# Packed attention and a gated convolution on one core: batch 0's first layer in two halves, its convolution off TensorE, more steps on GpSimd, other fillers, another order

## The chip, the cores and the metric

The kernel runs on one core of a Trainium2 chip, as one program in one launch. The metric is device time in microseconds, from the first instruction to the last. The kernel before takes 399.19 us (median of 3 runs, 398.37 to 400.52).

## The reference

Eight batches; attention has 8 heads of 576 positions and 64 channels, and 32 packed queries per head. What is computed, cut to what matters:

```python
p_packed = softmax(p @ k.T / 8) @ v          # 32 packed rows per head
x = softmax(q @ p_packed.T / 8) @ p_packed   # 576 rows per head, joined to 576 x 512 per batch
h = relu(x @ w_in)                           # 512 -> 1024
c = conv_w[0] * h[s-1] + conv_w[1] * h[s] + conv_w[2] * h[s+1]
out = (h * sigmoid(c)) @ w_out               # 1024 -> 512
```

q, k, v and p are float32; w_in, conv_w and w_out reach the kernel as 64-bit floats, which it rounds itself.

## The kernel before, in words

**Tiling.** The work is cut into 16 groups `g` of 4 heads (two per batch). For a group, `attention(g)` scores the packed queries against the keys, takes a softmax (`a1`), multiplies by `v`, turns the result (`ppT`), scores it against the queries and takes a second softmax in the tile `s2` (the profile writes `s`): VectorE turns it out of PSUM, takes maxima, subtracts them, ScalarE takes the exponential, VectorE sums, divides (a multiplication by the reciprocal) and turns it again. `packed_weight(b, hf)` multiplies the packed rows by `w_in`, so that the second attention product and the first layer become one product. `ffn1(b, j)` is that product for batch `b` and one of 8 blocks `j` of 128 channels. Then come a ReLU into a buffer `hbuf` (three of them), the three taps of the convolution, a tanh and a product into `hgt`. `ffn2(m)` multiplies 128 rows (36 tiles `m`, 4.5 per batch) by `w_out`; it first splits `hgt` into `xhi` and `xlo`.

**Two ways to multiply.** A float32 product on TensorE takes four passes over its columns, which the profile records as two matmuls. A split product writes each factor as a high and a low part in the one-pass format fp32r and adds three products (hi·hi, lo·hi, hi·lo). Before the change batch 0's first layer is float32 (tiles `a2f` and `gwf`, 4 instructions of 288 columns per `j`), and the other batches are split (`a2hi`, `a2lo`, `ghi`, `glo`, 12 instructions of 288 columns). In batch 0 the convolution of `j` = 0 is done by TensorE against three diagonal matrices (L903; GpSimd builds these, L497); all others are a tap on ScalarE (L927, one on VectorE, L923), two on VectorE (L929, L933), the tanh on ScalarE (L937) and the product on VectorE (L939). For the first two batches `glo` comes from TensorE: it adds minus the high part to the PSUM tile (L843).

**Who does what.** Names in the set `ON_DVE` put a step on VectorE where the function `either` would put it on ScalarE. Of the additions that round the weights, those not named there are done by GpSimd (L412, 512 columns each), each held by a dependency until the vector instruction before it in the program has ended.

**Order.** The string `ORDER` holds two characters per step: which stream's next step is issued. A planner made it beforehand from durations written into each `Step`. All engines work through their own queues in that order. `Flow` replays the plan while the program is built, and where it foresees that TensorE would wait, before the first tiles of the second layer, it puts in fillers (`warm(n)`, tile `idle`): matmuls whose result nobody reads. Loads are issued by SP, those of the first keys by ScalarE.

## Time and profile before

| | |
|---|---|
| median of 3 runs | 399.19 us |
| the profiled execution | 400.12 us; its span in the profile 398.3 us |
| TensorE (PE) busy | 390.3 us, 98% |
| VectorE (DVE) busy | 339.1 us, 85% |
| ScalarE (ACT) busy | 268.1 us, 67% |
| GpSimd (POOL) busy | 13.6 us, 3% |
| mean granted TensorE clock | 0.994 of full speed |

The 1.8 us between the span and the execution's time lie outside the recorded instructions. PE counts as busy from the start of a matmul to its modelled end, and matmuls overlap in the pipeline, so two further readings are needed: how long a run of matmuls lasts in the chain of work that ended last, and how busy the other engines are in the same stretch. A line such as L1058 is a line of the kernel before.

### The profile page before, as it was taken

The numbers are of one execution on the slowest core, as the hardware profiler recorded it, in microseconds if no ns is written. First come the engines' busy times: TensorE is split into PE (matmuls) and PEld (weight loads), VectorE is DVE, ScalarE is ACT, GpSimd is POOL, SyncE is SP. The second block draws the span as 40 slices with busy tenths as digits, with TensorE's granted clock in tenths as the row PEclk, the third lists the DMA queues.
The fourth block names the chain that finished last, engine by engine and source line by source line (L and its number), as shares of the span: only waits on it lengthen the run. The fifth ranks groups of instructions, "written<-read, shape, count | busy, mean of one in ns | idle before, by whom it ended". The sixth has DMA issues, their size and how long they took to land.

```text
span 398.3 us, 8049 instructions
## 1 busy us (share of the span) xinstructions
PE 390.3 (98%) x3281; PEld 310.6 (78%) x3281; DVE 339.1 (85%) x494; ACT 268.1 (67%) x430; POOL 13.6 (3%) x23
## 2 busy tenths in 40 slices
PE   6999999999999999999999999999999999999996
PEld 6767666678679789787788887989688878998885
DVE  3799999999999999999999899989976995887120
ACT  2599999887757577676846866757756667666221
POOL 1013112100000000000000000000000000000000
PEclk8999999999999999999999999999999999999999
DMA  8998899976989562976679626160000101001111
GB/s 274 358 371 256 199 309 149 185 105 106 168 153 152 107 96 54 143 140 94 156 108 157 162 28 156 19 114 26 28 26 28 53 2 53 28 0 54 53 53 54
DMA packets 157540, 47.60 MB, mean 120 GB/s; under 512 B 145460, under 2 KB 148788, under 8 KB 157504
## 3 DMA queue, kind: packets, MB, share of 16 engines
q1 hardware_dynamic: 157104, 46.41, 55.7%
q10 hardware_dynamic: 368, 0.66, 0.6%
q8 instruction: 26, 0.43, 0.5%
q14 instruction: 10, 0.08, 0.1%
q0 software_dynamic: 32, 0.02, 0.0%
HBM read 37.64 MB, written 9.44 MB: 118 GB/s over the span
## 4 chain that ended last, share of the span: by engine, by line
PE 88%; DMA 4%; DVE 3%; ACT 2%; SPq 1%; issue 1%; ACTq 0%; DVEq 0%
PE fo L1058 40%; PE big L880 23%; PE big L626 4%; PE sm L1058 4%; PE big L1008 4%; PE big L815 3%; PE sm L719 2%; PE big L710 2%; DMA hgt<-in_k_dram 2%; DMA p<-in_p_dram 1%; PE big L606 1%; SPq L676 1%; DMA out_dram<-o 1%; DVE hgt L929 1%; PE big L903 1%
## 5 line engine op out<-in xcount | busy, mean ns | idle before, releaser
L1058 PE MATMUL fo<-wo_hi,xhi 128*128 128x512 f32 x240 | 96.4, 402 | 0.4 <-ACT o L1073 0.4
L1058 PE MATMUL fo<-wo_lo,xhi 128*128 128x512 f32 x240 | 93.9, 391 | 0.0
L1058 PE MATMUL fo<-wo_hi,xlo 128*128 128x512 f32 x240 | 93.7, 390 | 0.0
L897 ACT ACTIVATE hbuf<-big 128x576 f32<-128x576 f32 x64 | 41.7, 653 | 40.5 <-PE big L880 40.3
L929 DVE SCALAR_TENSOR_TENSOR hgt<-hbuf,cw,hgt 128x576 f32<-128x576 f32 x63 | 50.5, 808 | 13.0 <-ACT hgt L927 12.2
L1031 DVE TENSOR_TENSOR xlo<-hgt,xhi 128x1024 fp32r<-128x1024 f32 (+1 forms) x38 | 41.6, 1102 | 18.3 <-ACT xhi L297 18.1
L1058 PEld LDWEIGHTS fo<-wo_hi,xhi 128*128 128x128 f32 x240 | 45.0, 188 | 14.4 <-issue 3.9
L937 ACT ACTIVATE hgt<-hgt 128x576 f32<-128x576 f32 x63 | 42.7, 683 | 18.4 <-DVE hgt L933 18.3
L1058 PEld LDWEIGHTS fo<-wo_hi,xlo 128*128 128x128 f32 x240 | 45.1, 188 | 10.1
L1058 PEld LDWEIGHTS fo<-wo_lo,xhi 128*128 128x128 f32 x240 | 45.1, 188 | 7.3
L933 DVE SCALAR_TENSOR_TENSOR hgt<-hbuf,cw,hgt 128x576 f32<-128x576 f32 x63 | 50.3, 805 | 0.6
L880 PE MATMUL big<-a2hi,ghi 128*128 128x288 f32 x224 | 49.7, 303 | 0.0
L927 ACT ACTIVATE hgt<-hbuf,cw 128x576 f32<-128x576 f32 x62 | 47.9, 777 | 1.0
L939 DVE SCALAR_TENSOR_TENSOR hgt<-hgt,hbuf 128x576 f32<-128x576 f32 x63 | 46.6, 750 | 2.0 <-ACT hgt L937 1.7
L880 PE MATMUL big<-a2lo,ghi 128*128 128x288 f32 x224 | 47.7, 294 | 0.0
L880 PE MATMUL big<-a2hi,glo 128*128 128x288 f32 x224 | 47.5, 293 | 0.0
L297 ACT CAST xhi<-hgt 128x1024 fp32r<-128x1024 f32 (+1 forms) x38 | 36.1, 954 | 10.9 <-PE fo L1058 4.9
L880 PEld LDWEIGHTS big<-a2hi,ghi 128*128 128x128 f32 x224 | 37.8, 188 | 6.0 <-ACT glo L297 0.5
L880 PEld LDWEIGHTS big<-a2hi,glo 128*128 128x128 f32 x224 | 35.8, 188 | 0.0
L880 PEld LDWEIGHTS big<-a2lo,ghi 128*128 128x128 f32 x224 | 35.8, 188 | 0.0
L1073 ACT COPY o<-fo 128x512 f32<-128x512 f32 x30 | 17.5, 584 | 22.2 <-PE fo L1058 18.4
L815 PE MATMUL big<-w_in_sb,ppT 64*32 64x512 f32 (+1 forms) x288 | 17.4, 547 | 0.5 <-ACT qT L297 0.5
(128 smaller groups left out, 551.8 us busy)
## 6 DMA issues: line engine op xcount, KB each, us to landing
out_dram<-o SPq DMA_DIRECT2D x35, 256.0 KB, 2.3
k<-in_k_dram SPq DMA_DIRECT2D x48, 144.0 KB, 4.1
q<-in_q_dram SPq DMA_DIRECT2D x48, 144.0 KB, 4.0
v<-in_v_dram SPq DMA_DIRECT2D x40, 128.0 KB, 3.1
hgt<-in_moe_w_in_dram SPq DMA_DIRECT2D x3, 1024.0 KB, 12.4
v<-in_v_dram SPq DMA_DIRECT2D x6, 512.0 KB, 9.4
hgt<-in_moe_w_out_dram SPq DMA_DIRECT2D x3, 1024.0 KB, 5.5
hgt<-in_q_dram SPq DMA_DIRECT2D x2, 576.0 KB, 6.8
```

Of the source, the lines that this page charges most:

```text
L297: nc.scalar.copy(out=out, in_=in_)
L815: nc.tensor.matmul(out=t[32 * c : 32 * c + 32, gg, :].rearrange("c (a f) -> c a f", f=DFF // 4), lhsT=grp[NG * b + gg]["ppT"][r, 32 * c : ...
L880: nc.tensor.matmul(out=t[:, hf, :SH], lhsT=w[:, gg, js], rhs=x[:, hf * SH : (hf + 1) * SH], start=n == 0, stop=n == (1 if b in F1F else 3) ...
L897: nc.scalar.activation(out=inner, in_=t[:, :, :SH], func=AF.Relu, scale=0.5)
L927: nc.scalar.activation(out=d, in_=h[:, 1 : S + 1], func=AF.Copy, scale=cw[:, NJ + j : NJ + j + 1])
L929: nc.vector.scalar_tensor_tensor(out=d, in0=h[:, 0:S], scalar=cw[:, j : j + 1], in1=d, op0=ALU.mult, op1=ALU.add)
L933: nc.vector.scalar_tensor_tensor(out=d, in0=h[:, 2 : S + 2], scalar=cw[:, 2 * NJ + j : 2 * NJ + j + 1], in1=d, op0=ALU.mult, op1=ALU.add)
L937: nc.scalar.activation(out=d, in_=d, func=AF.Tanh)
L939: nc.vector.scalar_tensor_tensor(out=d, in0=d, scalar=1.0, in1=h[:, 1 : S + 1], op0=ALU.add, op1=ALU.mult)
L1031: nc.vector.tensor_tensor(out=lo[:, js, o], in0=src[:, js], in1=hi[:, js, o].bitcast(F32), op=ALU.subtract)
L1058: nc.tensor.matmul(out=t, lhsT=x[:, c, :], rhs=w[:, c % 2, :], start=c + i == 0, stop=c == NJ - 1 and i == 2)
L1073: nc.scalar.copy(out=o, in_=t)
```

## The change

It does six things:

1. `F1F` becomes empty: batch 0's first layer is split as in the other batches. Each `j` has 12 one-pass instructions in place of 4 four-pass ones; `ghi` and `glo` are also made for batch 0 (8 more one-pass matmuls of 256 columns against `minus`, 4 more copies to `glo`), and so are `a2hi` and `a2lo` of its two groups.
2. `CONV_PE` becomes empty: the convolution of batch 0's `j` = 0 goes the way of all others; the 6 float32 matmuls and GpSimd's diagonal matrices are gone.
3. A set `ON_POOL` names the steps that GpSimd does: 8 additions of weights, 9 of the 16 subtractions and 13 of the 16 products in the second softmax, and 9 of the `xlo` subtractions of 1024 columns.
4. `ON_DVE` is another set: 8 ReLUs, 12 taps (before: one), `xhi` casts of 7 whole and 4 half tiles and 4 casts to `a2hi` are among what VectorE takes from ScalarE.
5. A filler is one single-pass matmul of 512 columns on zeros, in place of a float32 one of 128 columns on the identity. There are 29 of them; before there were 17.
6. `ORDER` is new, from a planner with other load times (three for the loads of weights, others for `v`) and a rule for turns between GpSimd and VectorE.

The new functions for quarter tiles (`quad_...`, `packed_again`) are not called, since `QUAD_K` and `QUAD_Q` are empty. Cut to its core, the diff is:

```diff
-    "3636363636000302360003356z073a0e046z05040a0534717101050a050c050c3b06340h3473093b050c0634700h053470050c0508347305"
+    "36350002003603013636036y346y3604076z366z0534040a0505700a3470340606050c053a3b0e09050h0c05340576720c05083b720d0h34"
...
-    FILL_NS, FILL_COLS, MARGIN = 216, 512, 100
+    FILL_NS, FILL_COLS, MARGIN = 226, 512, 100
...
-    ON_DVE = {"a1T0", "add20", "add21", "add30", "add40", "add50", "add51", "add70", "kT10", "kT15", "kT20", "qT00", "r0", "tap01"}
+    ON_DVE = {"gh000", "hi1", "hi10", "hi15", "hi5", "kT15", "qT05", "qT10", "r0", "relu45", "relu54", "relu64", "relu66", "relu67", "relu70", "relu73", "relu77", "tap02", "tap03", "tap31", "tap36", "tap40", "tap46", "tap56", "tap60", "tap64", "tap67", "tap70", "tap77", "x190", "x210", "x220", "x240", "x250", "x270", "x310", "x320", "x340"}
+    ON_POOL = {"add00", "add01", "add10", "add11", "add21", "add41", "add60", "add61", "mul0", "mul10", "mul11", "mul13", "mul14", "mul2", "mul3", "mul4", "mul5", "mul6", "mul7", "mul8", "mul9", "sub10", "sub13", "sub14", "sub3", "sub4", "sub5", "sub7", "sub8", "sub9", "xl20", "xl240", "xl260", "xl30", "xl330", "xl50", "xl60", "xl70", "xl80"}
-    F1F = (0,)
+    F1F = ()
-    CONV_PE = (0,)
+    CONV_PE = ()
...
+    nc.vector.tensor_copy(out=zeros, in_=stage[:, :128])
...
-            nc.tensor.matmul(out=t[:, :128], lhsT=ident, rhs=ident, start=True, stop=True)
+            nc.tensor.matmul(
+                out=t,
+                lhsT=zeros,
+                rhs=zeros.unsqueeze(1).broadcast_to([128, 4, 128]),
+                start=True,
+                stop=True,
+            )
...
+    def early_turn(key):
+        n = int("".join(c for c in key if c.isdigit()))
+        return n >= (40 if key[:3] == "add" else 4) or key[:2] == "xl"
...
+    def tensor_tensor(key, **kw):
+        if key not in ON_POOL:
+            nc.vector.tensor_tensor(**kw)
+            return
+        old = [i for i in nc.cur_bb.bb.instructions if i.engine == mybir.EngineType.DVE][-2 if early_turn(key) else -1]
+        added = nc.gpsimd.tensor_tensor(**kw)
+        tc.add_manual_dep(
+            added.ins,
+            old.name,
...
-        yield Step("SP", 2650 if i < 3 else 3500, after=after, sets=[("wd", i)])
+        yield Step("SP", (2650, 2650, 2650, 3200, 3200, 3600, 3600, 3600)[i], after=after, sets=[("wd", i)])
...
-        yield Step("DVE", 669)
-        nc.vector.tensor_tensor(
-            out=s3, in0=s3, in1=sm.unsqueeze(2).broadcast_to([128, SB, NP]), op=ALU.mult
+        yield either_pool(f"mul{g}", 1161, 669)
+        tensor_tensor(
+            f"mul{g}", out=s3, in0=s3, in1=sm.unsqueeze(2).broadcast_to([128, SB, NP]), op=ALU.mult
         )
```

**TensorE at the start.** These are its first instructions before: the seven early ones on `stage`, fillers, the turning of the first keys and queries, the first score (`kT,pT`) and the turning of the first softmax (`a_...`).

```order
L267 MATMUL idle<-stage 128x128 x7
L262 MATMUL idle<-ident 128x128
L606 MATMUL big<-ident,hgt_74 128x128 x5
L262 MATMUL idle<-ident 128x128 x2
L606 MATMUL big<-ident,hgt_74 128x128 x9
L626 MATMUL big<-kT,pT 32x288 x8
L606 MATMUL big<-ident,hgt_74 128x128 x9
L262 MATMUL idle<-ident 128x128 x9
L710 MATMUL big<-ident,a_168 128x128 x5
```

The same place in the changed kernel:

```order
L294 MATMUL idle<-stage 128x128 x7
L283 MATMUL idle<-zeros 128x512
L680 MATMUL big<-ident,hgt_75 128x128 x5
L283 MATMUL idle<-zeros 128x512 x2
L680 MATMUL big<-ident,hgt_75 128x128 x13
L700 MATMUL big<-kT,pT 32x288 x8
L283 MATMUL idle<-zeros 128x512 x5
L680 MATMUL big<-ident,hgt_75 128x128 x9
L283 MATMUL idle<-zeros 128x512 x2
L831 MATMUL big<-ident,a_174 128x128 x5
```

Between the first score and the first softmax's turning stand seven fillers in place of nine, and four more turned blocks stand ahead of the score.

**TensorE in batch 0's first layer.** Before, from the turning of group 3's packed rows (`sm<-ident,pb`) to the first tiles of the second layer (`big<-w`, with `hgt`):

```order
L735 MATMUL sm<-ident,pb 128x128
L262 MATMUL idle<-ident 128x128 x2
L626 MATMUL big<-qT,ppT 32x288 x8
L880 MATMUL big<-a2f,gwf 128x288 x4
L903 MATMUL big<-hbuf_76,hgt_74 128x288 x6
L815 MATMUL big<-w_in_sb,ppT 32x256 x8
L815 MATMUL big<-w_in_sb,ppT 32x512 x8
L880 MATMUL big<-a2f,gwf 128x288 x4
L843 MATMUL big<-ghi,minus 128x512 x2
L880 MATMUL big<-a2f,gwf 128x288 x4
L1008 MATMUL big<-w_717,hgt_74 128x512
```

After, from the fillers ahead of the same score on (the three rows on `a2hi` and `a2lo` stand twice for each `j`; one of the two is shown):

```order
L283 MATMUL idle<-zeros 128x512 x3
L700 MATMUL big<-qT,ppT 32x288 x8
L1010 MATMUL big<-a2hi,ghi 128x288 x2
L1010 MATMUL big<-a2lo,ghi 128x288 x2
L1010 MATMUL big<-a2hi,glo 128x288 x2
...
L945 MATMUL big<-w_in_sb,ppT 32x512 x8
L973 MATMUL big<-ghi,minus 128x256 x2
L1138 MATMUL big<-w_721,hgt_75 128x512 x4
```

The float32 rows and the convolution are gone, and the first fillers before that score are three in place of two. Of the 29 fillers, 19 stand between the first turned softmax and this score; before it were 5 of 17.

**GpSimd.** All that it adds before, up to its end:

```order
masks.py:199 AFFINE_SELECT ident<-ident 128x128
L412 TENSOR_TENSOR w_in_sb<-tmp 128x512 x4
L497 AFFINE_SELECT hgt_74<-cw 128x384
L412 TENSOR_TENSOR w_in_sb<-tmp 128x512
L412 TENSOR_TENSOR w_717<-tmp 128x512
L412 TENSOR_TENSOR tmp<-tmp 128x512 x3
```

After, the first twelve of its 39 (`s_...,sm` is a product, `s_...,mx` a subtraction of the second softmax):

```order
masks.py:199 AFFINE_SELECT ident<-ident 128x128
L325 TENSOR_TENSOR w_in_sb<-tmp 128x512 x2
L325 TENSOR_TENSOR s_288<-s_288,sm_355 128x576
L325 TENSOR_TENSOR w_in_sb<-tmp 128x512 x3
L325 TENSOR_TENSOR w_721<-tmp 128x512
L325 TENSOR_TENSOR s_775<-s_775,mx 128x576
L325 TENSOR_TENSOR s_583<-s_583,sm_796 128x576
L325 TENSOR_TENSOR tmp<-tmp 128x512
L325 TENSOR_TENSOR s_775<-s_775,sm_869 128x576
L325 TENSOR_TENSOR tmp<-tmp 128x512
L325 TENSOR_TENSOR xlo<-hgt_75,xhi 128x1024
```

Of the 31 steps that are new to GpSimd, 19 belong to groups up to 8 and to tiles up to 8 (13 in the softmax, 6 of `xlo`).

## Rows read from the trace of the kernel before

**Rows 1.** The page: span, and busy time of each engine with its share.

```profile
span 398.3 us, 8049 instructions
PE 390.3 (98%) x3281; PEld 310.6 (78%) x3281; DVE 339.1 (85%) x494; ACT 268.1 (67%) x430; POOL 13.6 (3%) x23
```

**Rows 2.** Busy time of each engine by stretch: length, then each engine, clock, DMA.

```profile
0.00:31.60 31.60, 27.85 (x380) 20.45 (x380) 21.68 (x43) 18.89 (x38) 5.46 (x16) 0.95 0.98 339
31.60:74.20 42.60, 42.54 (x361) 27.05 (x354) 41.79 (x67) 41.08 (x59) 6.85 (x6) 1.00 1.03 220
74.20:160.00 85.80, 85.79 (x765) 68.56 (x763) 85.09 (x122) 63.00 (x105) 1.30 (x1) 1.00 0.73 120
280.00:361.50 81.50, 81.50 (x547) 68.05 (x547) 66.02 (x88) 53.45 (x81) 0.00 (x0) 1.00 0.08 30
361.50:398.30 36.80, 32.98 (x169) 28.11 (x167) 9.05 (x11) 10.46 (x16) 0.00 (x0) 0.98 0.14 51
```

**Rows 3.** The page: the chain that ended last, shares of the span.

```profile
PE 88%; DMA 4%; DVE 3%; ACT 2%; SPq 1%; issue 1%; ACTq 0%; DVEq 0%
```

**Rows 4.** That chain in order of time: start, length, what.

```profile
1.25 6.66 DMA hgt<-in_k_dram
...
12.33 2.01 PE idle L262 x18
...
31.81 5.36 DMA p<-in_p_dram
...
44.29 2.91 PE big L903 x12
...
50.79 0.46 PE big L843 x2
51.26 1.94 PE big L880 x8
...
69.46 1.59 PE big L880 x12
...
84.24 1.39 PE fo L1058 x6
...
388.73 2.87 PE sm L966 x24
```

**Rows 5.** Groups by line and form: busy time, mean ns of one, idle before.

```profile
L762 DVE TENSOR_TENSOR s<-s,sm 128x576 f32<-128x576 f32 x16 | 12.0, 748 | 0.1
L749 DVE TENSOR_TENSOR s<-s,mx 128x576 f32<-128x576 f32 x16 | 11.9, 746 | 0.1
...
L1031 DVE TENSOR_TENSOR xlo<-hgt,xhi 128x1024 fp32r<-128x1024 f32 x30 | 36.4, 1214 | 18.3 <-ACT xhi L297 18.1
...
L923 DVE TENSOR_SCALAR hgt<-hbuf,cw 128x576 f32<-128x576 f32 x1 | 0.5, 521 | 0.0
...
L295 DVE COPY kT<-big 128x640 f32<-128x640 f32 x2 | 1.6, 808 | 0.0
...
L897 ACT ACTIVATE hbuf<-big 128x576 f32<-128x576 f32 x64 | 41.7, 653 | 40.5 <-PE big L880 40.3
L927 ACT ACTIVATE hgt<-hbuf,cw 128x576 f32<-128x576 f32 x62 | 47.9, 777 | 1.0
...
L297 ACT CAST xhi<-hgt 128x1024 fp32r<-128x1024 f32 x30 | 31.3, 1043 | 9.6 <-PE fo L1058 4.9 <-PE sm L1058 3.9 <-DVE hgt L939 0.8
...
L412 POOL TENSOR_TENSOR w_in_sb<-tmp 128x512 int32<-128x512 int32 x5 | 6.4, 1279 | 33.7 <-DVE tmp L459 16.6 <-DVE hgt L939 8.5 <-DVE s L762 6.6
```

**Rows 6.** Instructions in order of time, 18 to 34 us, GpSimd beside VectorE.

```profile
22.40 1.28 POOL L412 TENSOR_TENSOR w_in_sb<-tmp 128x512 int32<-128x512 int32 x1 [1.95 <-DVE s L749]
30.31 2.60 POOL L412 TENSOR_TENSOR w_in_sb<-tmp 128x512 int32<-128x512 int32 x2 [6.63 <-DVE s L762]
...
21.56 0.76 DVE L749 TENSOR_TENSOR s<-s,mx 128x576 f32<-128x576 f32 x1
22.42 0.76 DVE L694 TENSOR_REDUCE nm<-big 128x1 f32<-128x576 f32 x1
23.09 0.74 DVE L756 TENSOR_REDUCE sm<-s 128x18 f32<-128x576 f32 x1
...
29.41 0.74 DVE L762 TENSOR_TENSOR s<-s,sm 128x576 f32<-128x576 f32 x1
30.08 1.43 DVE L768 STREAM_TRANSPOSE a2f<-s 128x576 f32<-128x576 f32 x2
```

More of the change, by code (lines that the diff above doesn't have):

```diff
@@ L186, in run @@
                 self.free[engine], t = self.transfers(step, at)
-                end = (t, "DATA")
+                end = (t + step.late, "DATA")
             else:
+                if engine == "GP":
+                    before, last = self.vector
+                    at = max(at, (before if step.early else last)[1] + self.LAG["DVE"]["GP"])
+                    if last[2]:
+                        if last[0] + self.RACE <= at:
+                            at = max(at, last[1])
+                        elif at + step.ns > last[0]:
+                            self.free["DVE"] += at + step.ns - last[0]
+                    self.pool = at + step.ns
+                elif engine == "DVE":
+                    if step.two:
+                        at = max(at, self.pool)
+                    self.vector = [self.vector[1], (at, at + step.ns, step.two)]
                 end = (at + step.ns, engine)
@@ L438, in weight @@
         after = [("f2", m, i - 4) for m in range(F2F)]
-        yield Step("DVE", 1135, after=after, give=[token] * (not early), sets=[("w", i)] + [("wp", i)] * (src is st))
+        yield Step("DVE", 1135, two=True, after=after, give=[token] * (not early), sets=[("w", i)] + [("wp", i)] * (src is st))
         lo = wk.tile([128, 2, DM], F32R, name="wo_lo", tag="wo", bufs=8)
@@ L587, in head_transpose, with quad_transpose @@
         yield from half_transpose(g, name, 0, 5)
+    def quad_transpose(g, name, lo, hi):
+        nt = name + "T"
+        after = [(name, g)] + ([(nt + "p", g)] if lo else [e for k in range(max(g - 1, 0), g) for e in ready(nt, k)])
+        yield Step(
+            "DVE",
+            69 + 133 * (hi - lo),
+            after=after,
+            take=[nt] * (lo == 0),
+            give=["kq"] if lo and g >= NG else (),
+            sets=[(nt + "b", g)] if lo else [(nt, g), (nt + "p", g)],
+        )
+        if lo == 0:
+            grp[g][nt] = wk.tile([128, HG * SH], F32, name=nt, tag=nt, bufs=1)
+        cols = slice(lo * 128, hi * 128)
+        nc.vector.transpose(out=grp[g][nt][:, cols], in_=grp[g][name][:, cols])
     def half_transpose(g, name, lo, hi):
+        if quad(g, name):
+            yield from quad_transpose(g, name, lo, hi)
+            return
         nt = name + "T"
@@ L689, in attention @@
         G = grp[g]
-        yield Step("PE", 556, after=[("pT", g)] + ready("kT", g) + [("s1", g - 1)] * (g > 0), take=["big", "a1"], give=["kT"] + ["pT"] * (g % 4 == 3), sets=[("s1", g)], cols=1152, tiled=True)
-        t = score(G["pT"], G["kT"], g, [head(g, i) for i in range(HG)])
+        q4 = quad(g, "k")
+        yield Step("PE", 2000 if q4 else 556, after=[("pTq", 0) if q4 else ("pT", g)] + ready("kT", g) + [("s1", g - 1)] * (g > 0), take=["big", "a1"], give=["kT"] + ["pT"] * (g % 4 == 3), sets=[("s1", g)], cols=4608 if q4 else 1152, tiled=True)
+        heads = [head(g, i) for i in range(HG)]
+        if q4:
+            t = quad_score(packs["quad"], G["kT"], g, heads, g)
+        else:
+            t = score(G["pT"], G["kT"], g, heads)
         yield Step("DVE", 665)
@@ L913, in ffn1 @@
             )
-            yield Step("DVE", 729, give=["h"], sets=[("hg", b, j)])
+            yield Step("DVE", 669, two=True, give=["h"], sets=[("hg", b, j)])
             nc.vector.scalar_tensor_tensor(
@@ L920, in ffn1 @@
         key = f"tap{b}{j}"
-        yield either(key, 667, 371, after=under(b, j)) if b < 2 else Step("ACT", 667)
+        yield either(key, 667, 371, two=True, after=under(b, j))
         if key in ON_DVE:
```

261 lines of the change are left out of this document (169 added, 92 removed).

## The prediction

> **What bounds the kernel now.** The page comes first. TensorE is busy for 390.3 us of a span of 398.3 us, VectorE for 339.1, ScalarE for 268.1 and GpSimd for 13.6 [rows 1]. That alone does not say that TensorE is the bound, because a matmul counts as busy while it waits in the pipeline for the one ahead. The chain that ended last does: 88% of the span hangs on TensorE, 4% on transfers, 3% on VectorE and 2% on ScalarE [rows 3]. So time that TensorE does not have to spend is worth something, unless what feeds it has no time to give.
>
> That is read by stretches [rows 2]. In the first 31.6 us TensorE is busy for 27.85 us; this is the ramp, in which it waits for loads (the DMA engines are at 0.98) and for the first softmax. From 31.6 to 74.2 us, batch 0's first layer, all three engines are full: TensorE 42.54 of 42.60, VectorE 41.79, ScalarE 41.08. From 74.2 to 160 VectorE stays full (85.09 of 85.80) and ScalarE has room (63.00). From 280 to 361.5 VectorE has 15.5 us to spare, and in the last 36.8 us TensorE alone works, on tiles of the second layer that are left over. In the chain itself the ramp can be seen [rows 4]: 6.66 us for the load of the first keys, 2.01 us of fillers, and around 32 us a stretch of 5.36 us on the load of `p`; then TensorE row upon row.
>
> **TensorE's own work.** A `j` of batch 0's first layer takes 1.94 us as float32 (eight records) and 1.59 us split (twelve) [rows 4]. Eight of them save 8 x 0.35 = 2.8 us. The convolution on TensorE, 2.91 us [rows 4], goes. Against this stand 8 matmuls of 256 columns with `minus`. The nearest rows are 24 one-pass matmuls of 256 columns in 2.87 us, 0.12 us each, and two of 512 columns in 0.46 us [rows 4], so the eight cost 1.0 us. Net, the real work falls by 4.7 us.
>
> **The fillers.** Nine fillers took 2.01 us [rows 4], 0.223 us each, so 17 took 3.8 us. A new one is a one-pass matmul of 512 columns; six such matmuls of the second layer take 1.39 us [rows 4], 0.232 us each, so 29 take 6.7 us. That is 2.9 us more. A filler stands where the order foresees a wait. If the wait is real, the time would have passed without it too; if it is not, the filler makes one, since TensorE works in order. Either way the slot is used up. The bounds are 0 (all 2.9 us lie in time that already passes idle in the ramp, which is 31.6 - 27.85 = 3.75 us [rows 2]) and 2.9. I take 2.9: the new slots lie behind the first softmax, among chains that the shorter work on TensorE now meets earlier, and the idle of the ramp is mostly the load of the first keys, ahead of them. TensorE's sum is then -4.7 + 2.9 = -1.8 us.
>
> **ScalarE.** It gives away 8 ReLUs at 0.653, ten taps net at 0.777, 7 casts at 1.043 with 4 halves of that, and two `a2hi` casts of a ReLU's width [rows 5]: 5.2 + 7.8 + 9.4 + 1.3 = 23.7 us. It gets about five more copies out of PSUM, at the ReLU's 0.653, 3.2 us. Net 20.5 of 268.1 us, 7.6%. Most of it falls where ScalarE has room already. ScalarE holds 2% of the chain, 8.0 us [rows 3]; if its share shrinks as its work does, 0.6 us come off. The bounds are 0 and that.
>
> **VectorE.** To GpSimd go 13 products at 0.748, 9 subtractions at 0.746 and 9 `xlo` at 1.214 [rows 5], 27.4 us. It takes over 8 ReLUs out of PSUM: between 0.521 (the tap that it has, from SBUF) and 0.808 (640 columns from PSUM) [rows 5]; I scale the latter to 576 columns, 0.73, 5.8 us. Eleven more taps at 0.521 are 5.7. Whole `xhi` casts lie between 0.521 and that scaled to 1024 columns, 0.93; with the halves 4.7 to 8.3 us, and I take 6.5. Four `a2hi` are 2.1, and two `a2lo` and two taps for batch 0 some 3.0 by the 0.748 of a vector step of this width. In all 23 us come back, net -4.3. In the packed stretch it is better: 19 of the 31 new GpSimd steps are early, worth 13 x 0.747 + 6 x 1.214 = 17.0 us, while early additions to VectorE come to 6, net -11. I book nothing for it, since waits for GpSimd come with it.
>
> **GpSimd.** Its additions take 1279 ns for 512 columns [rows 5], 2.5 ns a column. By that a subtraction or product of 576 columns takes 1.44 us (twice VectorE's 0.748) and an `xlo` 2.56 us, 54.7 us in all 31, of which 34 early. What hides them: the chain of a group's softmax runs one or two groups ahead of TensorE, and TensorE meanwhile has second-layer tiles. Without that cover a group's two steps cost 2 x 0.7 us.
>
> **Sum.** -1.8 - 0.6 = -2.4 us. The profiled execution took 400.12 us, 0.9 over the median; I take the difference off the median of 399.19: **396.8 us**, -0.6%. The measurement can tell about 0.5% (2.0 us) from no change, so this lies just beyond it.
>
> **A rule that speaks against the change.** The rows show GpSimd's additions only beside vector steps with one operand [rows 6]: the one at 22.40 starts when a subtraction with two operands has ended (21.56 + 0.76), and the reductions beside it keep their 0.76 and 0.74 us; the pair at 30.31 starts after the product that ends at 30.15, beside turnings. No row has a two-operand vector step while GpSimd adds, so its price is unknown, between 0 and GpSimd's whole length. The Trainium skill's page "SBUF — State Buffer", section "Who interferes with whom", says that a vector instruction with two SBUF inputs, or in a two-port mode, contends with a GpSimd instruction that reads SBUF, and that whichever starts first makes the other wait to its end. By that rule taps, products and `xlo`, which is most of VectorE's load, could not run beside the 54.7 us above. The trace agrees as far as it goes.
>
> **The rivals.**
> - *All of the saving arrives.* The fillers lie in time that is idle anyway and VectorE's 11 us shorten waits. For it: VectorE holds 3% of the chain [rows 3]. Against it: 29 slots are more than 17. Then -4.7 - 0.6 = -5.3 us, 393.9.
> - *It does not reach the end.* From 31.6 to 74.2 us ScalarE has 1.5 us free and VectorE 0.8 [rows 2]. Batch 0 gives ScalarE four more copies to `glo` and VectorE two `a2lo`, so they may set the pace and TensorE wait where it worked. For it: the extra fillers, the full transfers (1.03). Against it: ScalarE gets free soon afterwards, and other tiles are there to fill. Then 399.2.
> - *GpSimd and VectorE shut each other out.* Place: up to 160 us, where VectorE has 0.7 us free in 85.8 [rows 2] and 34 us of new GpSimd work fall. If half of these 34 us hold VectorE up, 17 - 11 = 6 us arrive at TensorE, whose queue is in order: 396.8 + 6 = 402.8. It decides from 11 us on, a third of GpSimd's early time; the forecast's gain is gone at 13.4. Later the same loss would be covered by the 15.5 us of 280 to 361.5.
>
> **How the numbers follow.** Forecast (395 to 398) 0.45, all arrives 0.15, nothing arrives 0.23, shut out 0.17. Leaving out half of the shut-out cases and a few of the best, the range is 393.4 to 401.6; the forecast's own is 395 to 398. Faster by over 0.5% (under 397.2): nine tenths of the first, 0.40, and the second, 0.54 together, a hundredth rounded off. Slower: 0.17. Within 0.5%: the rest, 0.29.
>
> **What would show it.** Right: eight rows of twelve matmuls near 1.59 us for batch 0, 29 fillers of some 0.23 us each, TensorE's busy time near 388 us, ScalarE's near 248, VectorE's between 330 and 340, GpSimd's near 66, and the last stretch with TensorE alone of the same form. Fillers ending long after what the next matmul needs was ready would show that they cost time; vector taps of well over 0.81 us, or gaps in front of them that GpSimd's end closes, the shut-out. A granted clock under 1.00 behind the ramp, which has 0.95 now [rows 2], would show that the new fillers do not hold it. The prediction is wrong if waits of TensorE between 31.6 and 280 us grow or shrink by more than 2 us, which no row of before can settle.

## The result, and the profile after

The changed kernel takes 403.08 us (401.77 to 404.01, 6 runs) beside 398.52 for the kernel before (398.26 to 400.52, 6 runs): a ratio of 1.0104 with an interval of 1.0077 to 1.0130. It is 1.0% slower, and 1.5 us above the upper end of the forecast's range. The profiled execution took 402.67 us, its span is 400.9.

The page's busy line and the shares of its chain are the first to read (they answer to [rows 1, 3]):

```profile
PE 390.5 (97%) x3304; PEld 312.5 (78%) x3304; DVE 339.8 (85%) x502; ACT 249.4 (62%) x404; POOL 64.6 (16%) x52
...
PE 77%; DVE 11%; DMA 6%; SPq 2%; issue 2%; ACT 2%; POOL 0%; DVEq 0%; POOLq 0%; ACTq 0%
```

Busy times came out near the forecast: TensorE 390.5 (said: near 388), VectorE 339.8 (between 330 and 340), ScalarE 249.4 (near 248), GpSimd 64.6 (near 66). So the work that the change moves was counted about rightly, and the loss is to be looked for in time in which an engine waits. In the chain TensorE fell from 88 to 77%, VectorE rose from 3 to 11% and transfers from 4 to 6%.

Where the waiting lies is read by stretches (length, then PE, PEld, DVE, ACT, POOL, granted clock, DMA share, GB/s; they answer to [rows 2]):

```profile
0.00:31.60 31.60, 25.74 (x284) 18.80 (x284) 17.47 (x34) 17.32 (x33) 6.37 (x17) 1.00 0.97 328
31.60:74.20 42.60, 42.25 (x453) 27.88 (x453) 42.14 (x74) 42.05 (x67) 11.07 (x9) 1.00 0.93 224
74.20:160.00 85.80, 85.36 (x888) 66.77 (x887) 84.60 (x122) 64.86 (x107) 26.38 (x14) 1.00 0.82 157
280.00:361.50 81.50, 81.50 (x484) 68.71 (x483) 70.04 (x96) 40.47 (x62) 6.34 (x3) 1.00 0.07 27
361.50:400.90 39.40, 35.61 (x180) 30.29 (x178) 12.30 (x17) 7.93 (x13) 2.40 (x1) 0.98 0.15 54
```

The first stretch has it: TensorE is busy for 25.74 us of 31.6, after 27.85 before; VectorE fell from 21.68 to 17.47 and ScalarE from 18.89 to 17.32. All three engines start late. From 31.6 us on TensorE is as full as it was.

The first 14 us in order of time, ScalarE's instructions and the issues of loads (ACTq, SPq) with the first real work on TensorE:

```profile
0.73 1.28 ACT L518 ACT_TABLE_LOAD   x1 [0.73 <-PEq L1265]
...
1.19 0.48 SPq L619 DMA_DIRECT2D hgt<-in_q_dram  x1
...
1.71 0.44 SPq L582 DMA_DIRECT2D v<-in_v_dram  x1
...
2.22 0.31 POOL masks.py:199 TENSOR_SCALAR_AFFINE_SELECT ident<-ident 128x128 f32<-128x128 f32 x1
2.56 0.31 ACT L518 ACTIVATE minus<-ident 128x128 fp32r<-128x128 f32 x1 [0.54 <-POOL ident masks.py:199]
2.57 0.39 ACTq L602 DMA_DIRECT2D hgt<-in_k_dram  x1
...
3.00 0.66 ACTq L604 DMA_DIRECT2D hgt<-in_k_dram  x1
...
9.71 1.30 PE L680 MATMUL big<-ident,hgt 128*128 128x128 f32 x5 [4.44 <-DMA hgt<-in_k_dram]
```

This is the whole loss, as the experiments show. ScalarE's queue begins with its table load (0.73 to 2.01 us) and with `minus`, which waits for GpSimd to finish `ident` at 2.53 us. Behind them, in the same queue, stand the two issues of the first keys, at 2.57 and 3.00 us; of their delay 1.28 us are the table load and 0.54 the wait for `ident`. The first turning on TensorE starts at 9.71, after 4.44 us of waiting for those keys. In the kernel before, the first keys were ahead of `minus`: its second profile (last experiment) has their issues at 0.81 and 1.25 us and the first turning at 4.95. The chain shows it as one piece, beside one `j` of batch 0's first layer (start, length, what; they answer to [rows 4]):

```profile
2.57 7.00 DMA hgt<-in_k_dram
...
45.94 1.58 PE big L1010 x12
```

### The profile page after: what moved, and what is told of

Read it like the earlier page. It is cut to its first block, busy times and chain, and to the rows that moved or that the text cites. A ratio compares the mean times of both kernels' runs of the same rounds, so it can differ in the third digit from the quotient of the medians.

```text
span 400.9 us, 8143 instructions
## 1 busy us (share of the span) xinstructions
PE 390.5 (97%) x3304; PEld 312.5 (78%) x3304; DVE 339.8 (85%) x502; ACT 249.4 (62%) x404; POOL 64.6 (16%) x52
## 4 chain that ended last, share of the span: by engine, by line
PE 77%; DVE 11%; DMA 6%; SPq 2%; issue 2%; ACT 2%; POOL 0%; DVEq 0%; POOLq 0%; ACTq 0%
PE fo L1191 35%; PE big L1010 20%; PE sm L1191 4%; PE big L1138 4%; PE big L700 3%; DMA v<-in_v_dram 3%; PE big L945 3%; PE sm L840 2%; PE big L680 2%; DMA hgt<-in_k_dram 2%; PE idle L283 1%; SPq L628 1%; PE big L831 1%; DVE hgt L1063 1%; DVE hgt L1059 1%
## 5 line engine op out<-in xcount | busy, mean ns | idle before, releaser
L1059 DVE SCALAR_TENSOR_TENSOR hgt<-hbuf,cw,hgt 128x576 f32<-128x576 f32 x64 | 55.7, 877 | 5.1 <-ACT hgt L1057 4.8
L1010 PE MATMUL big<-a2hi,ghi 128*128 128x288 f32 x256 | 57.1, 304 | 0.1
L1027 ACT ACTIVATE hbuf<-big 128x576 f32<-128x576 f32 x56 | 36.4, 653 | 30.4 <-PE big L1010 30.0
L1010 PE MATMUL big<-a2lo,ghi 128*128 128x288 f32 x256 | 54.9, 295 | 0.0
L1010 PE MATMUL big<-a2hi,glo 128*128 128x288 f32 x256 | 54.9, 295 | 0.0
L1063 DVE SCALAR_TENSOR_TENSOR hgt<-hbuf,cw,hgt 128x576 f32<-128x576 f32 x64 | 52.0, 819 | 0.5
L1057 ACT ACTIVATE hgt<-hbuf,cw 128x576 f32<-128x576 f32 x52 | 40.1, 777 | 4.1 <-DVE hbuf L1025 3.3
L1010 PEld LDWEIGHTS big<-a2lo,ghi 128*128 128x128 f32 x256 | 41.1, 189 | 0.0
L325 POOL TENSOR_TENSOR xlo<-hgt,xhi 128x1024 fp32r<-128x1024 f32 x9 | 22.9, 2541 | 86.1 <-ACT xhi L337 60.6
L325 POOL TENSOR_TENSOR s<-s,sm 128x576 f32<-128x576 f32 x13 | 16.7, 1283 | 122.9 <-DVE sm L890 42.7
L322 DVE TENSOR_TENSOR xlo<-hgt,xhi 128x1024 fp32r<-128x1024 f32 (+1 forms) x29 | 30.6, 1066 | 6.1 <-ACT xhi L337 5.6
```

The source lines that it names most:

```text
L322: nc.vector.tensor_tensor(**kw)
L325: added = nc.gpsimd.tensor_tensor(**kw)
L1010: nc.tensor.matmul(out=t[:, hf, :SH], lhsT=w[:, gg, js], rhs=x[:, hf * SH : (hf + 1) * SH], start=n == 0, stop=n == (1 if b in F1F else 3) ...
L1027: nc.scalar.activation(out=inner, in_=t[:, :, :SH], func=AF.Relu, scale=0.5)
L1057: nc.scalar.activation(out=d, in_=h[:, 1 : S + 1], func=AF.Copy, scale=cw[:, NJ + j : NJ + j + 1])
L1059: nc.vector.scalar_tensor_tensor(out=d, in0=h[:, 0:S], scalar=cw[:, j : j + 1], in1=d, op0=ALU.mult, op1=ALU.add)
```

## The experiments

"Keys first" below is the changed kernel with that one thing mended; it is the base of most of the others. Where waiting on TensorE is given in sum, it is worked out from the starts of its matmuls: a group of like matmuls counts as work with the lower quartile of the times from its start to the next start, and what goes beyond is waiting. So summed, work and waiting on TensorE were, in us:

| kernel | work, fillers included | waiting | median |
|---|---|---|---|
| before, second profile | 372.8 | 18.6 | 398.7 |
| after | 370.7 | 25.2 | 403.08 |
| keys first | 370.6 | 20.2 | 397.81 |
| keys first, first layer not split | 373.0 | 19.2 | 399.19 |
| keys first, convolution on TensorE | 372.8 | 21.9 | 401.67 |

Medians of the kernel before in the four groups of runs were 398.7 to 398.9. The table's two columns are an estimate: grouping like matmuls in other ways moves more than a microsecond between them in the first row, while the differences among the last three rows change by half a microsecond at most.

### Keys first: `minus` behind the first keys

In `ORDER`, `00` is the load of the first keys (two steps), `35` the one that makes `minus`. TensorE's row order stays as it was.

```diff
-    "36350002003603013636036y346y3604076z366z0534040a0505700a3470340606050c053a3b0e09050h0c05340576720c05083b720d0h34"
+    "36000200353603013636036y346y3604076z366z0534040a0505700a3470340606050c053a3b0e09050h0c05340576720c05083b720d0h34"
```

> The changed kernel with one entry of its order moved: ScalarE makes the tile minus behind the two loads of the first keys, not ahead of them, so that these loads are issued some 1.8 us earlier (0.8 instead of 2.6 us). Theory late keys (the first keys come late, and the whole ramp hangs on them): 1.3 to 1.8 us faster than the changed kernel's 403.1, about 401.5, and the first turning of keys on TensorE starts near 8 us instead of 9.7. Theory shut-out (the loss lies in GpSimd and VectorE holding each other up, later in the program): under 0.5 us, 402.6 to 403.1. Theory fillers (the 29 slots are the loss): also under 0.5 us.

Measured: 397.81 us (397.56 to 398.35, 12 runs), ratio to before 0.9976 (0.9967 to 0.9985). The same instructions as above, in the new order:

```profile
0.75 0.41 ACTq L602 DMA_DIRECT2D hgt<-in_k_dram  x1
...
1.20 0.49 ACTq L604 DMA_DIRECT2D hgt<-in_k_dram  x1
...
1.72 1.28 ACT L518 ACT_TABLE_LOAD   x1 [1.72 <-PEq L1265]
...
3.02 0.31 ACT L518 ACTIVATE minus<-ident 128x128 fp32r<-128x128 f32 x1
...
5.06 1.25 PE L680 MATMUL big<-ident,hgt 128*128 128x128 f32 x5
```

The keys are issued 1.8 us earlier, and TensorE turns them 4.65 us earlier, at 5.06. That is worth 5.3 us (5.0 between the two profiled executions), all of the loss and more, and several times the 1.8 us by which the issue moved, which the expectation took for the whole gain; why late keys are that late is taken up below. The stretches of this kernel:

```profile
0.00:31.60 31.60, 29.54 (x366) 21.05 (x369) 22.51 (x46) 22.30 (x41) 7.91 (x18) 1.00 0.99 332
31.60:74.20 42.60, 42.40 (x405) 28.49 (x405) 42.16 (x68) 42.10 (x65) 9.52 (x7) 1.00 0.92 221
```

TensorE is busy for 29.54 us of the ramp, and the clock is at 1.00.

### Keys first, and the first values late

The first load of `v` (`01`) goes behind the second keys (`07`).

```diff
-    "36000200353603013636036y346y3604076z366z0534040a0505700a3470340606050c053a3b0e09050h0c05340576720c05083b720d0h34"
+    "360002003536033636036y346y360407016z366z0534040a0505700a3470340606050c053a3b0e09050h0c05340576720c05083b720d0h34"
```

> As the run with the keys first, and SP also issues the first load of v behind the second group's keys, as the kernel before does, so that the first keys share the DMA engines with less. Theory late keys: the first turning of keys starts near 5.3 us as before, and the time falls by the whole 4 us that separate 9.7 from there, less what another wait takes: 399.5 to 400.5. Theory shut-out and theory fillers: 402.5 to 403.1 still.

Measured: 399.67 us (399.43 to 399.97), 1.9 us worse than keys first, ratio to before 1.0020 (1.0011 to 1.0028). The first turning starts at 5.07, so taking the values away from behind the keys doesn't bring the keys earlier. That the time lies in the range of the theory of late keys is luck: keys first alone has their whole gain.

Nor is the 1.9 us the price of late values: the first product with them starts at 13.92 us, only 0.28 later than in keys first. With this order the plan puts in 38 fillers in place of 29, and eight of them stand ahead of the turning of the next keys, `k`:

```profile
14.75 2.11 PE L283 MATMUL idle<-zeros 128*128 128x512 f32 x8
...
16.70 0.71 PE L680 MATMUL big<-ident,k 128*128 128x128 f32 x5
```

`k` was issued at 4.88 us and had landed at 14.73. In keys first it is turned from 14.47 on, as soon as it is there; here the eight fillers stand in its way for 1.95 us. The plan foresaw a wait that wasn't there, and the fillers made one. The same order without them was not run.

### The kernel before with its keys late

The opposite edit, in the kernel before: `35` in second place.

```diff
-    "3636363636000302360003356z073a0e046z05040a0534717101050a050c050c3b06340h3473093b050c0634700h053470050c0508347305"
+    "3635363636360003023600036z073a0e046z05040a0534717101050a050c050c3b06340h3473093b050c0634700h053470050c0508347305"
```

> The kernel before with one entry of its order moved: minus (and so the load of ScalarE's table) ahead of the loads of the first keys. Theory late keys: 1.3 to 1.8 us slower than before, 400.0 to 400.3, the converse of the first run. Theories shut-out and fillers: like before, within 0.5 us.

Measured: 403.73 us (402.87 to 403.99), ratio 1.0116 (1.0099 to 1.0133), 5.0 us more than before where 1.3 to 1.8 were expected. The place of one entry in the order, with none of the change's other parts, costs as much as the mended entry gave back:

```profile
2.61 0.42 ACTq L553 DMA_DIRECT2D hgt<-in_k_dram  x1
...
9.63 1.33 PE L606 MATMUL big<-ident,hgt 128*128 128x128 f32 x5 [4.40 <-DMA hgt<-in_k_dram]
```

### No fillers, with late keys and with early ones

In the changed kernel, and then in keys first, `warm` issues nothing; the seven early matmuls on `stage` stay.

```diff
-        for _ in range(n):
+        for _ in range(0):
```

> The changed kernel without its 29 fillers (the seven early matmuls stay); no result depends on them. Theory fillers (they take time that TensorE could use): up to 2.9 us faster, 400.2 to 402. Theory late keys and theory shut-out: the fillers stand in real waits, within 0.5 us of 403.1. If the fillers hold the granted clock, it falls below 1.00 in the ramp and the time gets longer by a microsecond or more.

> The changed kernel with the first keys' loads ahead of `minus` (397.8 us) and no fillers behind the seven at the start. Theory 1, fillers take the place of waits for the most part: without the 29 it saves about the 1.0 us that leaving them out saved with the keys late, 396.8. Theory 2, the order's waits are real once the keys come early, so the fillers cost nothing: 397.8. Theory 3, they hold the clock: a granted clock under 1.00 from 31.6 us on and 399 or more. Theory 4, the prediction's term: they use up their whole slot, so 6.7 us go and 391 comes out.

Measured: 402.06 us (401.25 to 402.81) with late keys, 1.0 less than with fillers, clock at 1.00 in the profiled execution, and just outside the ranges of both theories; and 398.59 us (397.47 to 399.28) with early ones, 0.8 more than with fillers, ratio to before 0.9987 (0.9977 to 0.9998). Both differences are small beside the spread: each time the runs with and without fillers overlap. In the second, the clock of the first stretch is 0.96 and of the next 0.99:

```profile
0.00:31.60 31.60, 23.00 (x325) 16.48 (x325) 22.25 (x45) 21.89 (x39) 7.89 (x18) 0.96 0.98 329
31.60:74.20 42.60, 41.37 (x414) 28.32 (x411) 41.34 (x68) 41.58 (x64) 9.50 (x7) 0.99 0.88 213
```

With the keys where they belong, the 29 fillers earn some 0.8 us (0.6 if each kernel is held against the kernel before of its own group). Of the four theories none holds alone: the nearest is that they cost nothing and hold the clock, by less than said.

### The 31 steps back on VectorE

From keys first, `ON_POOL` loses its 13 products, 9 subtractions and 9 `xlo` and keeps the eight additions.

```diff
...
+    ON_POOL = {"add00", "add01", "add10", "add11", "add21", "add41", "add60", "add61"}
```

> The changed kernel with the first keys' loads ahead of `minus` (397.8 us), and the 31 steps that the change gave to GpSimd (13 products, 9 subtractions, 9 `xlo`) back on VectorE; GpSimd keeps its eight additions. Theory 1, GpSimd relieves VectorE: 27 us come back to VectorE, some 17 of them before 160 us, where it has no time to spare, and at least a tenth of that reaches TensorE: 399.5 or more. Theory 2, GpSimd and VectorE shut each other out, so that the 31 steps cost more than they give: 396.8 or less, with the taps back at 0.81 us. Theory 3, VectorE's time does not reach the end: 397.4 to 398.2.

Measured: 410.45 us (410.13 to 411.19), ratio 1.0290 (1.0272 to 1.0308): 12.6 us more than keys first. Theory 1 holds, far beyond its least. VectorE's busy time is 358.8 after 339.8, and TensorE, full in both stretches in keys first, is no longer so:

```profile
74.20:160.00 85.80, 81.39 (x821) 62.89 (x828) 85.62 (x124) 59.99 (x101) 0.00 (x0) 0.98 0.79 150
160.00:280.00 120.00, 117.65 (x1031) 96.00 (x1019) 115.27 (x169) 76.01 (x125) 0.00 (x0) 1.00 0.42 87
```

TensorE loses 4.0 and 2.35 us here against keys first (85.38 and 120.00). Summed by starts, its waiting is 28.8 us after 20.2, and its work 374.7 after 370.6. Of that work a part is the clock, 0.98 from 74 to 160 us, and a part are fillers: planned with these durations the kernel has 40 of them in place of 29. At 0.24 us each, as the eight of the run with the first values late took (1.95 us), the eleven are at most 2.7 us by estimate, so that some 10 us are left for the 31 steps. The order was laid out for GpSimd's help, so this is the price of taking it away from this order, not from the best one without it.

### The kernel before without its convolution on TensorE

In the kernel before, `CONV_PE` is empty; a tap on ScalarE and two on VectorE stand in its place, and the fillers that the order would add there are left out, so that there are 17 as before.

```diff
-    CONV_PE = (0,)
+    CONV_PE = ()
```

> The kernel before (398.7 us) with the convolution of batch 0's first tile taken from TensorE alone: one tap on ScalarE and two on VectorE in its place, everything else in the order of before, as many fillers as before. Theory 1, the prediction's term: TensorE is the bound there, so the 2.9 us of the convolution are saved, 395.8. Theory 2, the convolution stood where TensorE would have waited, so that a wait takes its place: 398.2 to 399.0. Theory 3, VectorE, which is full there, gets 1.6 us more and passes it on: 400.

Measured: 400.63 us (399.83 to 401.31), ratio 1.0041 (1.0024 to 1.0057): slower by 1.75 us, past the 400 of theory 3, and not for its reason, since VectorE is no busier in the stretch (41.73 us after 41.79). The stretch, what stands where the convolution stood, and the same cast to `ghi` in the kernel before:

```profile
31.60:74.20 42.60, 39.74 (x335) 24.27 (x334) 41.73 (x66) 39.97 (x57) 5.08 (x4) 0.96 1.03 220
```

```profile
44.46 0.78 ACT L927 ACTIVATE hgt<-hbuf,cw 128x576 f32<-128x576 f32 x1
...
48.09 1.02 ACT L297 CAST ghi<-big 128x1024 fp32r<-128x1024 f32 x1
...
49.16 0.74 PE L843 MATMUL big<-ghi,minus 128*128 128x512 f32 x2 [2.28 <-ACT ghi L297]
```

```profile
48.77 1.01 ACT L297 CAST ghi<-big 128x1024 fp32r<-128x1024 f32 x1
```

TensorE is busy for 39.74 of 42.6 us, 2.8 less than in [rows 2]: just the convolution's 2.91 is missing, and time stays. It now waits 2.28 us for the cast to `ghi`. In the kernel before the cast follows the products that it takes up (L815) at once, 48.77 after 48.66 us; here these end at 44.75, and ScalarE comes to the cast at 48.09, behind work to which a tap of 0.78 us was added. In the old order the convolution filled a wait. The clock of the stretch, 0.96 after 1.00, makes it dearer: of the six runs the one with a mean clock of 1.00 took 399.83 us, those at 0.994 and 0.995 took 400.85 to 401.31.

### The first keys on SyncE's queue

The order of the changed kernel is left as it is; the keys' two loads are issued by SyncE.

```diff
-                nc.scalar.dma_start(out=t[:, :640], in_=rows[:, :640])
+                nc.sync.dma_start(out=t[:, :640], in_=rows[:, :640])
```

> The changed kernel with its order untouched, `minus` ahead of the first keys, but the two loads of the first keys issued by SyncE in place of ScalarE; there they stand behind the load of `p` and around that of the first queries. Theory 1, ScalarE's queue holds the loads back until GpSimd's `ident` is there: SyncE does not wait for that, the first turning on TensorE begins at 5.5 us or sooner after 9.7, and the time is 397.5 to 399. Theory 2, it is `minus` or the table load itself that is in the wrong place (or another part of the new order that the late keys go with): 402 to 403.

Measured: 398.24 us (397.51 to 399.62), ratio 0.9984 (0.9972 to 0.9996); the keys are issued at 1.19 and 2.18 us and first turned at 5.07. `minus` and the table load stand where the change put them, and the loss is gone: it was the queue.

### Late keys, and the values behind the second keys

From the changed kernel, `01` goes behind `07`.

```diff
-    "36350002003603013636036y346y3604076z366z0534040a0505700a3470340606050c053a3b0e09050h0c05340576720c05083b720d0h34"
+    "363500020036033636036y346y360407016z366z0534040a0505700a3470340606050c053a3b0e09050h0c05340576720c05083b720d0h34"
```

> The changed kernel with its order kept (`minus` ahead of the first keys), but SyncE's first load of values moved behind the second keys. It tests why keys issued 1.8 us later are used 4.4 us later. Theory 1, sharing: the loads that SyncE issued meanwhile (0.6 MB of queries and 0.5 MB of values) go ahead of the late keys; without the values the first turning on TensorE begins 1.2 us or more sooner, at 8.5 or earlier after 9.71. Theory 2, the keys' own load got slower for another reason: it still begins at 9.5 to 9.8. The time says little here, since the values were worth 1.9 us where the keys came first: 401.5 to 404.

Measured: 404.48 us (404.32 to 404.63), ratio 1.0143 (1.0128 to 1.0159). The first turning comes no earlier:

```profile
1.71 0.44 SPq L619 DMA_DIRECT2D hgt<-in_k_dram  x1
...
2.19 0.43 SPq L582 DMA_DIRECT2D v<-in_v_dram  x1
...
2.57 0.39 ACTq L602 DMA_DIRECT2D hgt<-in_k_dram  x1
...
9.60 1.30 PE L680 MATMUL big<-ident,hgt 128*128 128x128 f32 x5 [4.33 <-DMA hgt<-in_k_dram]
```

That doesn't tell the theories apart after all: the second keys, 576 KB, are now issued at 1.71 us, and the values, 512 KB, at 2.19, still ahead of the first keys' 2.57. More is ahead of the first keys than before, and they land no later (6.89 us after their issue; in the changed kernel 7.00). The kernel is 1.4 us slower than the changed one, and the trace shows what was met above: 38 fillers, eight of them from 19.51 to 21.48 us ahead of a `k` that had landed at 14.69.

### All of SyncE's loads as late as the keys

From the changed kernel: the first queries wait on SyncE for `minus`, and with them every load behind them.

```diff
-        nc.scalar.mul(out=minus, in_=ident, mul=-1.0)
+        packs["minus"] = nc.scalar.mul(out=minus, in_=ident, mul=-1.0)
...
+                if g == 0:
+                    tc.add_manual_dep(
+                        added.ins,
+                        packs["minus"].ins.name,
```

> The changed kernel with its order kept (`minus` ahead of the first keys on ScalarE), and the first queries made to wait on SyncE for `minus`, so that every load behind them on SyncE goes out some 1.8 us later as well, and the late keys are again ahead of the queries and values, as they are where the keys come first. Theory 1, sharing: keys issued at 2.57 us are slow (7.0 us to landing, 3.7 where they come first) because loads issued ahead of them have the transfer engines; with those held back they land in 4.5 us or less, the first turning on TensorE begins at 7.1 us or sooner after 9.71, and the time is 1.8 to 2.4 us above that of keys first: 399.4 to 400.3. Theory 2, what is late is late by itself: the first turning at 9 us or later and 403 or more.

Measured: 399.94 us (399.04 to 400.75), ratio 1.0028 (1.0019 to 1.0037). The keys are issued at 2.57 as in the changed kernel:

```profile
2.57 0.39 ACTq L602 DMA_DIRECT2D hgt<-in_k_dram  x1
2.90 0.35 SPq L619 DMA_DIRECT2D hgt<-in_q_dram  x1
...
3.29 0.44 SPq L582 DMA_DIRECT2D v<-in_v_dram  x1
...
6.45 1.30 PE L687 MATMUL big<-ident,hgt 128*128 128x128 f32 x5 [1.18 <-DMA hgt<-in_k_dram]
```

Now the first half of the keys lands 3.7 us after its issue, as in keys first, where it took 7.0 in the changed kernel; the turning starts at 6.45 us after 9.71. Making 0.6 MB of queries, 0.5 MB of values and all that follows them later gave 3.1 us back. That is sharing: in the changed kernel 2.36 MB are moved from the issue of the first half, 320 KB, to its landing, most of them for SyncE's loads. By what rule the engines divide their time isn't shown; 0.6 MB more ahead of the keys (the run above) made them no later. The Trainium skill has a sentence that bears on this on its page "DMA: Bandwidth & Descriptors", section "Issuing engines are not separate DMA queues": transfers run on the same 16 engines and interleave there, whichever engine issued them. The runs agree, and give the price: 1.8 us at the issue became 4.65 us at the first use.

### Convolution and split undone, each by itself

From keys first: the convolution of `j` = 0 back on TensorE with 27 fillers (the order loses two steps of the taps and gains the diagonals' one); and in another kernel the first layer in float32 again (the order loses the steps to `a2lo`, `glo` and `minus`).

```diff
-    CONV_PE = ()
+    CONV_PE = (0,)
```

```diff
-    F1F = ()
+    F1F = (0,)
```

> The changed kernel with the first keys' loads ahead of `minus` (397.8 us), and the convolution of batch 0's first tile put back on TensorE (its diagonals on GpSimd, no tap on ScalarE and two vector taps fewer), everything else in the same order; 27 fillers after 29. Theory 1, the prediction's term holds once the new order is there: TensorE is the bound in that stretch, 2.9 us more, 400.4 to 400.8. Theory 2, the convolution lies in time that TensorE waits anyway, as in the kernel before without it: 397.3 to 398.3. Theory 3, VectorE and ScalarE set the pace there and get 2.4 us back: 396.5 or less.

> The changed kernel with the first keys' loads ahead of `minus` (397.8 us), and batch 0's first layer in float32 again: eight matmuls for each of its tiles, none of the eight matmuls with `minus`, four copies to `glo`, two casts to `a2hi` and two `a2lo` fewer; the rest in the same order. Theory 1, the prediction's terms: 8 x 0.35 = 2.8 us more on TensorE, 1.0 of it back from `minus`: 399.4 to 399.8. Theory 2, the copies that go were what held batch 0's first layer up, since ScalarE and VectorE are full there: 397.5 or less. Theory 3, the rest of the order was laid out for the shorter first layer, so that others wait as well: 400.5 or more.

Measured: 401.67 us (401.43 to 402.14) with the convolution, 3.9 more than keys first and past the range of theory 1, since besides 2.2 us of work 1.7 us of waiting come in (table); and 399.19 (398.35 to 400.07) without the split, 1.4 more, just under the range of theory 1. The stretch of batch 0's first layer in the two, the convolution's first:

```profile
31.60:74.20 42.60, 41.54 (x399) 27.89 (x398) 37.44 (x63) 37.80 (x59) 10.00 (x8) 1.00 0.91 222
```

```profile
31.60:74.20 42.60, 42.60 (x364) 25.98 (x362) 39.91 (x65) 40.04 (x60) 8.89 (x7) 1.00 0.94 225
```

The signs are the prediction's. With the convolution VectorE and ScalarE have 5 us free there (37.44 and 37.80 of 42.6), so their load doesn't end the stretch. In float32 TensorE is full (42.60 after 42.40 in keys first), with less waiting in sum (table): of the 2.4 us of work that the split takes off TensorE, 1.0 us comes back as waiting.

### The kernel before, profiled a second time

> The kernel before, unchanged, profiled a second time. Its first profile shows a granted clock of 0.50 from 8 to 10 us, behind a wait of 1.47 us for the second half of the first keys, and took 400.12 us, 1.4 over its median. Theory 1, that fall of the clock is a matter of the single execution: here the clock stays at 1.00 in 6 to 12 us, the nine turnings that took 2.18 us take 1.6 or less, and the time is 398.3 to 399.1. Theory 2, the fall belongs to the kernel and the 1.4 us come from elsewhere: the clock falls again.

Measured: 398.36 us, clock 1.00. The same two microseconds in its first profile and in this one, and the nine turnings in each; the first profile is shown first:

```profile
8.00:10.00 2.00, 2.00 (x9) 1.73 (x9) 0.85 (x2) 0.59 (x1) 0.00 (x0) 0.50 1.04 388
```

```profile
8.00:10.00 2.00, 1.87 (x28) 1.17 (x27) 1.65 (x3) 0.59 (x1) 0.00 (x0) 1.00 1.04 386
```

```profile
7.95 2.18 PE L606 MATMUL big<-ident,hgt 128*128 128x128 f32 x9 [1.47 <-DMA hgt<-in_k_dram]
```

```profile
7.37 1.20 PE L606 MATMUL big<-ident,hgt 128*128 128x128 f32 x9 [1.26 <-DMA hgt<-in_k_dram]
```

In the first profile the clock stood at its lower level, 0.50 of full speed, after TensorE had run out of fillers and stood still for 1.47 us waiting for the second half of the first keys. In the second it waited 1.26 us and kept its clock. The nine turnings cost 2.18 us in the one and 1.20 in the other. So the first profile's 400.12 us held 1.4 us that the median of 398.7 doesn't. The other executions bear out that it is the clock: of the 78 of the kernel before in the four groups, five had a mean clock of 0.993 to 0.995 and took 399.66 to 400.45 us; the others had 0.998 or more and took 398.03 to 399.40 us. Why the clock falls in some of them isn't shown.

## Why the prediction was wrong, by its own steps

**The step that failed** is the sentence in which fillers were costed: "the idle of the ramp is mostly the load of the first keys, ahead of them". It took that idle, the 3.75 us of [rows 2] with the 6.66 us of [rows 4], as given, and went on to what lies behind it; a later start of that load was put at nothing, without a reason. The change moves an instruction ahead of that load. The prediction named the load of the first keys as the first piece of the chain, and looked at the new order of TensorE and GpSimd; ScalarE's queue, from which this load is issued, was not looked at. Shown: that one entry is worth +5.3 us in the changed kernel (403.08 against 397.81) and +5.0 in the kernel before.

**With that mended**, the change gives -0.9 us (398.74 to 397.81, beside before in the same runs) where -2.4 was said. The level of 397.81 lies in the forecast's own 395 to 398, helped by a base of 398.7 where the forecast had 399.19, but little over a third of the gain arrives. By the sums over TensorE:

- *TensorE's own work and the fillers* were booked at -4.7 + 2.9 = -1.8 us. Its work, fillers included, fell by 2.2 (372.8 to 370.6; by other groupings 0.7 to 3.2). Undone singly, the split is 2.4 us of work and the convolution, beside two fillers fewer, 2.2, so the -4.7 was about right. In batch 0 a split `j` takes 1.58 to 1.79 us in the chain (1.59 forecast), and there are 29 fillers:

```profile
L283 PE MATMUL idle<-zeros x29: 389/397/795, 4.5 to 51.3; 128*128 128x512 f32 x29
```

- *The fillers* were mis-sized. The upper bound of 2.9 us more was taken; in this order they belong at the lower bound, since leaving all of them out saves nothing with early keys. The upper bound does exist: eight fillers put where nothing was to wait for cost 1.95 us (keys first, and the first values late).
- *Waiting* was not booked, and rose by 1.6 us (18.6 to 20.2; by other groupings 0.1 to 2.6). By each of three groupings it falls by 1 to 2 us in the first 30 us, where fillers stand in waits, rises by some 2 us in batch 0's first layer (from 30 to 70 us TensorE waits 4.2 us after 2.1) and by some 1 us from 70 to 160. From 30 to 280 us it grew by 1.8 to 3.3 us; more than 2 was the prediction's own sign that it is wrong. This is the rival "it does not reach the end" in part. Its place was right (ScalarE 42.10 and VectorE 42.16 of 42.6 us), and undoing the split takes 1.0 us of the waiting away.
- *The convolution* had a price of 2.9 us in every order by the prediction. Taken off alone in the old order it made the kernel 1.75 us slower, some of it by the clock, put back alone in the new one 3.9 us slower: it covered a wait of 2.28 us in the one, and in the other it stands in TensorE's way. One row's duration isn't its price.
- *ScalarE's* -0.6 us was not tested by itself.
- *VectorE* was to come out at -4.3 us and came out at +0.7, with nothing booked. The taps were stretched, L1059 to a mean of 877 ns from 808 and L1063 to 819 from 805, 64 of each, together 5.3 us, nearly all of it in four taps (below).

**The shut-out rival** gave 402.8 us, close to the result, and is not its cause. What it says does happen. The first rows are of the taps L1059 and L1063 in all of the kernel after (shortest, median, longest ns); the next two show one of them beside GpSimd:

```profile
L1059 DVE SCALAR_TENSOR_TENSOR hgt<-hbuf,cw,hgt x64: 719/810/3000, 41.9 to 363.8; 128x576 f32<-128x576 f32 x64
```

```profile
L1063 DVE SCALAR_TENSOR_TENSOR hgt<-hbuf,cw,hgt x64: 759/810/1599, 42.9 to 364.7; 128x576 f32<-128x576 f32 x64
```

```profile
136.67 2.41 POOL L325 TENSOR_TENSOR xlo<-hgt,xhi 128x1024 fp32r<-128x1024 f32 x1 [3.32 <-ACT hgt L1057]
136.70 3.00 DVE L1059 SCALAR_TENSOR_TENSOR hgt<-hbuf,cw,hgt 128x576 f32<-128x576 f32 x1 [0.20 <-ACT hgt L1057]
```

The tap takes 3.00 us where its median is 0.81. It starts 0.03 us behind GpSimd's `xlo` and ends at 139.70, 0.62 us after GpSimd's end at 139.08. This is the rule that was weighed in the prediction, from the Trainium skill's page "SBUF — State Buffer", section "Who interferes with whom": the one that started first makes the other wait to its end. The row agrees, but for the last tenths: what the tap takes behind GpSimd's end, 0.62 us, is less than the shortest tap's 0.72. It happens to four of the 128 taps: this one, one of 1.31 us at 153.72, one of 2.55 at 307.83 and, of L1063, one of 1.60 at 209.36, 5.2 us over the median in all, 2.7 of them up to 160 us. Where a vector step with both inputs in SBUF starts first, it keeps its length and GpSimd's step is the longer one: products and subtractions that take 1.16 us by the median take 1.5 to 1.7, an `xlo` of 2.41 takes 2.8. Beside a step with one input in PSUM (`glo` at 109.01 us) a product keeps its 1.16. Each of GpSimd's steps is placed behind a chosen vector step; without that placing nothing was run. Without the 31 steps these taps are short again,

```profile
L1059 DVE SCALAR_TENSOR_TENSOR hgt<-hbuf,cw,hgt x64: 721/809/822, 37.2 to 371.4; 128x576 f32<-128x576 f32 x64
```

and the kernel is 12.6 us slower, eleven more fillers included. Taps held up cost VectorE 5.2 us, and with these counted the 31 steps take 19 us of busy time off it (358.8 to 339.8). That the 31 steps help, given the order made for them, is shown. Which instructions would run if the order had been planned without them isn't.

**GpSimd's** durations were a little better than worked out, 1.16 us for a product (said 1.44) and 2.41 for an `xlo` (said 2.56), by the medians:

```profile
L325 POOL TENSOR_TENSOR s<-s,sm x13: 1157/1159/1602, 27.4 to 302.7; 128x576 f32<-128x576 f32 x13
...
L325 POOL TENSOR_TENSOR xlo<-hgt,xhi x9: 2399/2413/2859, 79.3 to 376.0; 128x1024 fp32r<-128x1024 f32 x9
```

What stays open: how the 0.9 us divides to the tenth between work, fillers and waiting, and how much of the 2.7 us by which taps are held up before 160 us reaches TensorE.

## What to carry to other kernels

When an order is replaced, compare the first instructions of every queue that issues a transfer, the compute engines' included: an instruction that is long or waits for another engine (here a table load of 1.28 us and a wait of 0.54), put ahead of an issue, delays a load, and no busy time shows it. A load that goes out a little late can come in very late if other queues meanwhile keep the transfer engines busy; it can pay to hold those back. Where a plan puts in fillers, count them in every variant: three of the edits above brought 9 to 11 more, and in two of these they were the loss. Price a removed instruction by what its engine would do in its place, not by its length, and profile the base twice where the expected gain is as small as one fall of the clock.

## What the runs showed that was not expected

- Keys issued 1.82 us later (2.57 after 0.75) were used 4.65 us later; with the other loads held back, 1.39 us later (6.45 after 5.06).
- Delaying loads made a kernel faster: 403.08 to 399.94 us.
- A wait of TensorE at the same place of the same kernel, 1.47 us long in one execution and 1.26 in another, was followed by a granted clock of 0.50 in the one and of 1.00 in the other; the first took 1.4 us more than the median.
- Of the 31 steps on GpSimd all but a few ran without holding VectorE up: four of 128 taps bore 5.2 us of it.
- GpSimd took 1.16 us for 576 columns with a broadcast operand and 2.41 us for 1024 columns, 2.0 and 2.4 ns a column, after 2.5 for its additions.
